# Sums of v over four blocks at a time, in a kernel that mixes a Fourier layer with sliding-window attention

## The chip, the cores and the metric

The kernel runs on one core of one Trainium2 chip. The metric is the device time of one execution in microseconds (us). Engines are named as the profile names them: PE is TensorE (PEld its weight loads), DVE VectorE, ACT ScalarE, POOL GpSimd, SP SyncE, whose queue issues most DMAs.

## The reference

The input x has 2048 rows of 512. Two mixers work on it, and a gate of each row blends them:

```python
g = sigmoid((x * gate_w).sum(-1))                     # one number for each row
a = x @ dft_hid_re.T ;  b = x @ dft_hid_im.T
y = dft_seq_re @ a - dft_seq_im @ b                   # Fourier mixer, 2048 x 2048 matrices
q, k, v = split(x @ wqkv)                             # 32 heads of 16
p = softmax(q @ k.T / 4, over the last 256 rows)      # causal sliding window
out = g * y + (1 - g) * ((p @ v) @ wo)
```

All of it is float32. The kernel splits each factor of a dense product into a rounded high part and a rest, and multiplies high by high, high by rest and rest by high (`TERMS`), so each dense product costs three matmuls.

## The kernel before

**Two streams on TensorE.** The order of TensorE's instructions is written by hand; that of the other engines and of the DMA queues is made by a scheduler, except where the code pins an instruction: `behind("sp")` issues what follows not before the last instruction that was marked on that queue, and `late(...)` the same for ScalarE and VectorE. The *dense stream* (`dense`, a generator) gives one 128 x 512 matmul at a time: projections of q, k and v for head group 0, of q and k for groups 1 to 3, the b projections (between groups 1 and 2) and the a projections of x (after group 3), then the products with the 2048 x 2048 matrices (`c_block`, "dc"), and near the end the output projection (`wo_block`). The *attention stream* is the loop over n at the end. It has 4 head groups x 32 blocks of 64 rows = 128 blocks. In step n, for four pairs p of a group's heads, it issues

- `s_pair(n, p)`: S, scores of queries against 320 keys. VectorE adds the mask and takes the row extreme (L329), ScalarE does the exponential and its sum (L332);
- `t_pair(k, p)` with k = n - LAG: T, the same scores transposed, with the row maxima as additional rows of the contraction. ScalarE takes the exponential into the tile `pt` (L393), GpSimd clears what lies outside the window (L398, L402);
- `pv`: the sums of v, products of `pt` with a padded v (`vpad`), four matmuls of 32 columns side by side for each block and bank (L419, "o"). I call a run of them a *visit*;
- between these, `fill(n)` lets matmuls of the dense stream in, 3.0 to 3.6 for each call pair.

S, T and the maxima's transposes share four PSUM banks (`ps_a`).

**Rings and pads.** q and k are stored to DRAM by the projections (`qk_scr`) and loaded 512 rows at a time into two ring tiles (`ring_load`, four DMAs). `ring_ahead` decides in which step: for group g and part ss the load waits for n - LAG >= 32 (g - 1) + 8 ss + 9, so that T no longer needs the rows that are overwritten. `make_pad` cuts a block out of a ring into a pad tile, one block ahead of its use; there are NPAD pads of each kind.

**Maxima and row sums.** After each eight blocks `m_rows` transposes their maxima on TensorE (L339), VectorE splits them, a DMA stores them (`m_scr`), and a second DMA, which waits for the first, loads them into four rows of the q ring for T. `l_rows` does the like for the row sums.

**v.** `v_load` loads v of four blocks into a raw tile, two steps later `v_spread` has GpSimd copy it into `vpad`, and three steps after that the first block of the four is summed.

**The gate.** `gate_load` loads 256 rows of x, `gate` multiplies them with gate_w and sums over the row on VectorE (L211).

Of the kernel before, what the change touches and what calls it, by code (L numbers as in the profile page):

```python
# [14 lines left out]
P = 128  # L15
# [9 lines left out]
SCALE = 0.25  # L25
LAG = 18
WARM = 6
BEHIND = 4
# [4 lines left out]
def fnet_window_mix(ctx: ExitStack, tc: tile.TileContext, xT, x, wqk, wv, wr, wi, cr, ci, wo, gw, out):  # L33
# [21 lines left out]
    def ld(dst, src):  # L55
        return nc.sync.dma_start(dst, src)

    def store(dst, src):
        mark("sp", ld(dst, src))

# [64 lines left out]
    def pt_raw():  # L125
        return at.tile([P, NP, WIN], F32, name="pt", bufs=3).rearrange("p a b -> p (a b)")[:, :1024]

    with tc.manual_schedule(engines={mybir.EngineType.Activation, mybir.EngineType.DVE, mybir.EngineType.SP}):
        wraw, *xraw = [pt_raw() for _ in range(3)]
        wq0 = [st.tile([P, 1024], F32R, name=h) for h in ("hi", "lo")]  # L130
        zero = at.tile([P, 512], F32R, name="rl", bufs=1)
        nc.vector.memset(f(zero[:]), 0.0)
        for dk in (0, 2, 1, 3):
            XRAW[dk, 0] = xraw[dk // 2][:, HALVES[dk % 2]]
            if dk % 2 == 0:
                nc.scalar.dma_start(XRAW[dk, 0], xT[0, dk])
        for dk in range(DK):
            store(wraw[:, dk * 256:dk * 256 + 256], wqk[0][:, dk * 256:dk * 256 + 256])
            if dk % 2 == 0:
                ld(XRAW[dk + 1, 0], xT[0, dk + 1])  # L140
        for dk in range(DK):
            c = slice(dk * 256, dk * 256 + 256)
            mark("act", nc.scalar.copy(wq0[0][:, c], wraw[:, c]))
            split_x(0, (dk,), dk > 0)
            mark("dve", nc.vector.tensor_sub(wq0[1][:, c], wraw[:, c], f(wq0[0][:, c])))


    NPAD = 3
    pads = [[const.tile([P, NP, P], F32R, name=f"pad{i}_{b}") for b in range(NPAD)] for i in range(2)]
# [14 lines left out]

    half = const.tile([P, 2], F32, name="half")
    mrow = const.tile([P, 2], F32, name="mrow")
    for t, edges in ((half, ((0, 16, 32, 48, 64, 80), (16, 32, 48, 64, 80, 96))), (mrow, ((96, 98), (98, 100)))):
# [13 lines left out]
    clear_rows(0, 0)  # L181
    vpad = [const.tile([P, 4, NP, 32], F32, name=f"vpad{b}") for b in range(2)]

# [12 lines left out]
    g0 = const.tile([P, 16], F32, name="g0")  # L196
    gwb = const.tile([P, D], F32, name="gwb")

    GX = {}

    def gate_load(j):
        if j == 0:
            with behind("sp"):
                ld(gwb, bass.AP(tensor=gw.tensor, offset=gw.offset, ap=[[0, P], [1, D]]))
        GX[j] = st.tile([P, 1024], F32, name="raw", bufs=2)
        for c in range(2):
            ld(GX[j][:, HALVES[c]], x[2 * j + c])

    def gate(tb):
        t = GX[tb // 2][:, HALVES[tb % 2]]  # L210
        nc.vector.scalar_tensor_tensor(t, t, 1.0, gwb, op0=OP.mult, op1=OP.mult,  # L211
                                       accum_out=gl[:, tb:tb + 1])
        if tb == 15:
            e = const.tile([P, 16], F32, name="ge")
            nc.scalar.activation(e, gl, AF.Exp, scale=-1.0)
            nc.vector.tensor_scalar_add(e, e, 1.0)
            nc.vector.reciprocal(g1, e)
            nc.vector.tensor_scalar(g0, g1, -1.0, 1.0, op0=OP.mult, op1=OP.add)
# [4 lines left out]
    def qk_evict(g, ss, i, ps):  # L223
        hl = ev.tile([P, 2, 512], F32R, name="hl", bufs=2)
        split_psum(hl[:, 0], hl[:, 1], ps, -SCALE if i == 0 else 1.0)
        store(qk_scr[i][g][ss].rearrange("h x s -> x h s"), f(hl[:]))

# [46 lines left out]
    def v_proj(sb, w):  # L274
        ps = ps_d.tile([P, 512], F32, name="dv", tag="d")
        yield from row_proj(sb, w, ps)
        t = ev.tile([P, 512], F32, name="ev")
        mark("act", nc.scalar.copy(t, ps))
        store(v_scr[sb // 2][sb % 2].rearrange("r a g x -> r (a g x)"), t)
        yield  # L280
# [6 lines left out]
    def ab_proj(i, sb, w, dst=None):  # L287
        ps = ps_d.tile([P, 512], F32, name="dab", tag="d")
        yield from row_proj(sb, w, ps)
        if dst is None:  # L290
            hl = ev.tile([P, 2, 512], F32R, name="hl", bufs=2)
            split_psum(hl[:, 0], hl[:, 1], ps, 1.0 if i == 0 else -1.0)
            store(ab_scr[i][sb], f(hl[:]))
        else:
            split_psum(dst[:, 0], dst[:, 1], ps)
        yield
# [38 lines left out]
    def m_rows(u):  # L335
        U = u % 4
        nm = ML[u][0]
        pt = ps_a.tile([P, 512], F32, name="s", tag="st")
        nc.tensor.matmul(pt[:32, :P], nm, ident, start=True, stop=True)  # L339
        hl = at.tile([32, 2, 2, 64], F32R, name="mhl", bufs=1)  # L340
        m = pt[:32, :P].rearrange("c (a r) -> c a r", a=2)
        nc.vector.tensor_scalar(hl[:, :, 0], m, -1.0, None, op0=OP.mult)
        nc.vector.scalar_tensor_tensor(hl[:, :, 1], m, -1.0, f(hl[:, :, 0]), op0=OP.mult, op1=OP.subtract)
        ld(m_scr[u].rearrange("x p (j r) -> (p j) x r", r=64), f(hl[:]).rearrange("c a h r -> c (a h) r"))
        ld(f(ring[0][96:100, :, U * 512:(U + 1) * 512]), m_scr[u])

    def l_rows(u):
        l = ML.pop(u)[1]
        nc.vector.reciprocal(l, l)
        pt = ps_a.tile([P, 512], F32, name="s", tag="st")  # L350
        nc.tensor.matmul(pt[:32, :P], l, ident, start=True, stop=True)  # L351
        lt = at.tile([32, P], F32, name="lt", bufs=1)
        nc.vector.tensor_copy(lt, pt[:32, :P])
        for a in range(2):
            ls = l_scr[u]
            ld(bass.AP(tensor=ls.tensor, offset=ls.offset + a * 512, ap=[[1024, NP], [64, 8], [1, 64]]),
               lt[:, 64 * a:64 * a + 64])
# [7 lines left out]
    def v_load(n):  # L365
        if n >= NG * NB:
            return
        g, kb = divmod(n, NB)
        raw = at.tile([P, 4, 64], F32, name="vr")
        for h in range(2):  # L370
            ld(raw[64 * h:64 * h + 64].rearrange("r (c j) x -> r c j x", j=2),
               v_scr[kb // 4][:, :, h, g, :].rearrange("c (j r) x -> r c j x", r=64))
        VR[n] = raw

    def v_spread(n):
        if n >= NG * NB:
            return
        raw = VR.pop(n)
        v2 = vpad[n // 4 % 2]
        for h in range(2):  # L380
# [4 lines left out]
    def t_pair(n, p):  # L385
        q0 = n % NB * BQ
        w = min(WIN, S - q0)
        if p == 0:
            PT[n] = at.tile([P, NP, WIN], F32, name="pt", bufs=3)
        pt = PT[n]  # L390
# [101 lines left out]
    def dense():  # L492
        warm()
        with behind("sp"):
            wraw = [load_raw(wv[i]) for i in range(2)]
        qk_first(wq0)
        wvs = [late(split_raw, r, True) for r in wraw]
        load_x(1, 0)
# [20 lines left out]
        for g in range(1, NG):  # L519
            for ss in range(4):  # L520
                yield from qk_proj(g, ss, w)
                have.add(("qk", g, ss))
                if g == 1:
                    if ss == 0:
                        wraw.append(load_raw(wi[1]))
                    elif ss < 3:
# [3 lines left out]
                        if ss == 1:  # L530
                            raw = load_raw(wqk[2])
                        else:
                            gate_load(0)
                elif g == 2:
# [10 lines left out]
            if g == 1:  # L545
                for sb in range(16):
                    yield from ab_proj(1, sb, ws)
                    if sb == 1:
                        nextw = late(split_raw, raw)
                    if sb % 2 == 0 and sb < 14:  # L550
                        gate_load(sb // 2 + 1)
                    if sb % 2:
                        late(gate, sb - 1)
                        late(gate, sb)
            if g < 3:
                w = nextw
        ab = {}
        for sb in range(16):
            if sb >= 4:
                ab[sb] = big.tile([P, 2, 512], F32R, name="big")  # L560
            yield from ab_proj(0, sb, ws, ab.get(sb))
        for sc in range(4):
            ab[sc] = load_ab(0, sc)
# [109 lines left out]
    ctx.enter_context(tc.manual_schedule(engines={mybir.EngineType.PE}))  # L673
    N = NG * NB
    need(("qk", 0, 0))
    ring_ahead(0)
    need(("v", 5))

    for n in range(N + LAG + 2):
# [6 lines left out]
        ring_ahead(n + 1)  # L686
        if -4 <= k < N - 4 and k % 4 == 0:
            for c in range(2):
                need(("v", (k + 4) % NB // 2 + c))
            with behind(*(("sp",) if k < 4 else ())):  # L690
                v_load(k + 4)
        if -4 <= k and k % 4 == 2:
            v_spread(k + 2)
        if n == 0:
            make_pad(0, 0)
        for p in range(NP):
# [9 lines left out]
            fill(n)  # L706
            if p == 2 and n % 2:
                for j in (k - 2, k - 1):
                    if 0 <= j < N:
                        pv(j)  # L710
                if n % 8 == 1 and 1 < n <= N + 1:
                    m_rows(n // 8 - 1)
                    l_rows(n // 8 - 1)
    attention_done()
# [46 lines left out]
```

## Time and profile before

| | us |
|---|---|
| median of three runs | 878.73 (878.17 to 880.12) |
| the profiled execution | 880.74 |
| its span, first to last instruction | 878.9 |
| PE busy | 868.7 (99%) |
| DVE busy | 601.4 (68%) |
| ACT busy | 583.6 (66%) |
| POOL busy | 386.6 (44%) |

The profile is of one execution. A row of a group or of the timeline names the line, the engine, the operation and the tiles (out<-in). In the timeline the first column is the start and the second the length; matmuls are pipelined and their lengths modelled, so it is the distance from start to start that tells TensorE's pace. A stretch's row (`A:B`) gives its length, the busy time of PE, PEld, DVE, ACT and POOL, the granted clock of TensorE, the DMA engines' busy share and GB/s.

### The profile page before, as it was taken

What the parts mean: (1) busy time and instruction counts of PE and PEld (TensorE: products, weight loads), DVE (VectorE), ACT (ScalarE), POOL (GpSimd) and SP (SyncE); (2) the same over time, 40 slices, a digit from 0 to 9 for tenths busy, and PEclk for the clock granted to TensorE, in tenths of its full rate; (3) what the DMA queues carried; (4) which work ended last, traced back from release to release, by engine and by line L of the source; (5) the groups of instructions that cost most, each with busy time, mean ns of one, the idle gap of its engine ahead of it and who ended that gap; (6) DMA issues with size and microseconds to landing.
All of it is one profiled execution on the core that took longest, in us unless ns stands there. A gap on an engine that the chain in (4) does not pass through costs nothing.

```text
span 878.9 us, 17233 instructions
## 1 busy us (share of the span) xinstructions
PE 868.7 (99%) x5190; PEld 694.0 (79%) x5190; DVE 601.4 (68%) x1968; ACT 583.6 (66%) x1793; POOL 386.6 (44%) x1069
## 2 busy tenths in 40 slices
PE   8999989999999999999999999999999999999998
PEld 6888867777878778787878787878787777788886
DVE  3588969777888678777877677878686434644341
ACT  3478978879898887888887878888786444110000
POOL 9100246454544447665456565645656665100000
PEclk9999999999999999999999999999999999999999
DMA  6877678675676126635445454469842425565531
GB/s 227 264 216 200 203 230 264 233 256 194 185 241 215 44 71 210 166 111 146 140 137 134 138 152 134 129 193 332 267 155 94 139 85 171 174 201 173 181 120 48
DMA packets 90541, 153.17 MB, mean 174 GB/s; under 512 B 26832, under 2 KB 35792, under 8 KB 90448
## 3 DMA queue, kind: packets, MB, share of 16 engines
q1 hardware_dynamic: 90016, 151.42, 55.1%
q8 instruction: 41, 0.67, 0.3%
q10 hardware_dynamic: 432, 0.66, 0.2%
q14 instruction: 52, 0.43, 0.2%
HBM read 104.33 MB, written 47.71 MB: 173 GB/s over the span
## 4 chain that ended last, share of the span: by engine, by line
PE 97%; DMA 1%; DVE 0%; issue 0%; ACT 0%; DVEq 0%; ACTq 0%
PE dc L450 41%; PE dab L268 10%; PE s L327 9%; PE dqk L246 9%; PE o L419 8%; PE t L392 8%; PE dv L268 5%; PE t L638 5%; DMA qk_scr<-hl 1%; PE s L234 1%; PE s L351 0%; DMA pt<-xT 0%; PE s L339 0%; ACT pt L393 0%; DVE lo L84 0%
## 5 line engine op out<-in xcount | busy, mean ns | idle before, releaser
L450 PE MATMUL dc<-big,hi 128*128 128x512 f32 x1024 | 354.8, 395 | 0.0
L398 POOL TENSOR_SCALAR_AFFINE_SELECT pt<-pt 64x128 f32<-64x128 f32 x512 | 194.3, 379 | 291.1 <-ACT pt L393 275.2
L332 ACT ACTIVATE sm<-sm,nm 128x320 f32<-128x320 f32 (+4 forms) x512 | 276.8, 542 | 56.8 <-DVE nm L329 54.1
L329 DVE CUSTOM_DVE_ANT_0 sm<-s,mask 128x320 f32<-128x320 f32 (+4 forms) x512 | 232.3, 462 | 114.9 <-PE s L327 88.5
L393 ACT ACTIVATE pt<-t 128x320 f32<-128x320 f32 (+4 forms) x512 | 207.9, 412 | 76.0 <-PE t L392 73.9
L450 PEld LDWEIGHTS dc<-big,hi 128*128 128x128 f32 x1024 | 186.9, 188 | 27.8 <-issue 1.5
L450 PE MATMUL dc<-big,lo 128*128 128x512 f32 x512 | 202.6, 396 | 0.0
L402 POOL TENSOR_SCALAR_AFFINE_SELECT pt<-pt 64x128 f32<-64x128 f32 x448 | 161.1, 360 | 0.0
L327 PE MATMUL s<-ring,pad 128*128 128x320 f32 (+4 forms) x512 | 160.4, 313 | 0.0
L392 PE MATMUL t<-ring,pad 128*128 128x320 f32 (+4 forms) x512 | 154.5, 302 | 2.9 <-ACT pt L393 2.9
L312 DVE TENSOR_SCALAR pad<-ring,half 96x256 fp32r<-96x256 f32 x384 | 121.8, 359 | 19.6 <-PE t L392 19.2
L327 PEld LDWEIGHTS s<-ring,pad 128*128 128x128 f32 x512 | 96.2, 188 | 38.7 <-issue 8.8
L392 PEld LDWEIGHTS t<-ring,pad 128*128 128x128 f32 x512 | 96.2, 188 | 20.4 <-ACT pt L393 4.0
L450 PEld LDWEIGHTS dc<-big,lo 128*128 128x128 f32 x512 | 96.2, 188 | 16.4 <-issue 1.6
L84 DVE TENSOR_TENSOR lo<-raw,hi 128x512 fp32r<-128x512 f32 x146 | 99.6, 713 | 0.0
L332 ACT ACTIVATION_READ_ACCUMULATOR sm<-sm,nm 128x1 f32 x512 | 98.2, 192 | 0.0
L268 PE MATMUL dab<-hi,big 128*128 128x512 f32 x256 | 92.1, 400 | 0.0
L83 DVE CAST hi<-raw 128x512 fp32r<-128x512 f32 x142 | 56.5, 438 | 43.4 <-PE dc L450 42.6
L246 PE MATMUL dqk<-big,hi 128*128 128x512 f32 x240 | 85.9, 393 | 0.0
L419 PE MATMUL o<-pt,vpad 128*32 128x320 f32 (+4 forms) x1408 | 78.5, 353 | 0.0
L81 ACT CAST os<-ev 128x512 fp32r<-128x512 f32 x16 | 9.8, 621 | 84.9 <-DMA ev<-o_scr 80.7
L419 PEld LDWEIGHTS o<-pt,vpad 128*32 128x32 f32 x1408 | 35.9, 109 | 37.2 <-issue 20.1
(83 smaller groups left out, 827.8 us busy)
## 6 DMA issues: line engine op xcount, KB each, us to landing
qk_scr<-hl SPq DMA_DIRECT2D x32, 512.0 KB
ring<-qk_scr SPq DMA_DIRECT2D x32, 512.0 KB
raw<-cr SPq DMA_DIRECT2D x32, 512.0 KB
raw<-ci SPq DMA_DIRECT2D x32, 512.0 KB
ab_scr<-hl SPq DMA_DIRECT2D x20, 512.0 KB
big<-ab_scr SPq DMA_DIRECT2D x20, 512.0 KB
ring<-qk_scr SPq DMA_DIRECT2D x32, 256.0 KB
r_scr<-ev SPq DMA_DIRECT2D x27, 256.0 KB
```

The costliest lines, as they stand in the source:

```text
L246: nc.tensor.matmul(ps, w[a][:, c:c + 128], XT[dk, ss][:, b], start=n == 0, stop=n == 11)
L268: nc.tensor.matmul(ps, XT[dk, ss][:, a, c * 128:(c + 1) * 128], wh[b], start=n == 0, stop=n == 11)
L312: nc.vector.tensor_scalar(dst, src, half[:96, h:h + 1], None, op0=OP.mult)
L327: nc.tensor.matmul(ps[:, :w], PAD[0, n][:, p], ring[1][:, p, k0:k0 + w], start=True, stop=True)
L329: mark("dve", nc.vector.tensor_tensor_reduce(out=sm[:, :w], in0=ps[:, :w], in1=mask[:, WIN - w:], scale=1.0, scalar=3e38, op0=OP.add, op1= ...
L332: mark("act", nc.scalar.activation(sm[:, :w], sm[:, :w], AF.Exp, bias=nm[:, c], scale=-1.0, accum_out=l[:, c]))
L392: nc.tensor.matmul(ps[:, :w], PAD[1, n][:, p], ring[0][:, p, q0:q0 + w], start=True, stop=True)
L393: nc.scalar.activation(pt[:, p, :w], ps[:, :w], AF.Exp, scale=-1.0)
L398: nc.gpsimd.affine_select(a, a, pattern=[[0, 2], [1, 64]], compare_op=OP.is_ge, fill=0.0, base=0, channel_multiplier=-1)
L402: nc.gpsimd.affine_select(a, a, pattern=[[0, 2], [-1, 64]], compare_op=OP.is_gt, fill=0.0, base=0, channel_multiplier=1)
L419: nc.tensor.matmul(OT[g, sb][32 * p:32 * p + 32, q - sb * 512:e - sb * 512], v2[:, p], pt[:, p, q - q0:e - q0], start=first, stop=kb == 8 ...
L450: nc.tensor.matmul(ps, w[a][:, s8 * 128:(s8 + 1) * 128], ab[SC[i]][:, b], start=i == 0 and a + b == 0, stop=i == 15 and a == 1)
```

## The change

- **Visits.** The sums of v are made at p = 2 of each step with k a multiple of 4, four blocks at a time, where before they were made at odd n, two blocks at a time. `pt` has five buffers instead of three.
- **LAG** is 21 instead of 18: T runs 21 blocks behind S.
- **Room** for it: NPAD 2 instead of 3, one `vpad` instead of two, one raw v tile instead of two; the small tile of the row sums and the gate's weights come out of the pool `ev`; `half` and `mrow` share a tile; the DMA scratch is 512 bytes instead of 1024.
- **v loads** for blocks k to k + 3 are issued in step n = k + LAG (before: those for k + 4 to k + 7), all pinned behind SP's last DMA. Every load is now marked on SP's queue, not only the stores.
- **Maxima.** The load of the maxima into the ring is issued from ScalarE's queue, one step after the visit in which they were transposed, pinned behind ScalarE's last marked instruction.
- **Gate.** Its loads and products move from the b projections, two products at each second of 16 row blocks, to the a projections, two products at each of the row blocks 2 to 9.
- **Start.** WARM is 8 instead of 6, and the v weights' splits stand ahead of the first q and k projection's evictions (ScalarE's order is now: four casts of the v weights, then the two evictions).

```diff
-LAG = 18
-WARM = 6
+LAG = 21
+WARM = 8
...
     def ld(dst, src):
-        return nc.sync.dma_start(dst, src)
-
-    def store(dst, src):
-        mark("sp", ld(dst, src))
+        mark("sp", nc.sync.dma_start(dst, src))
...
-    NPAD = 3
+    NPAD = 2
...
-    vpad = [const.tile([P, 4, NP, 32], F32, name=f"vpad{b}") for b in range(2)]
+    vpad = [const.tile([P, 4, NP, 32], F32, name="vpad")]
...
         if j == 0:
+            gwb.append(ev.tile([P, D], F32, name="ev"))
             with behind("sp"):
-                ld(gwb, bass.AP(tensor=gw.tensor, offset=gw.offset, ap=[[0, P], [1, D]]))
+                ld(gwb[0], bass.AP(tensor=gw.tensor, offset=gw.offset, ap=[[0, P], [1, D]]))
...
-        ld(f(ring[0][96:100, :, U * 512:(U + 1) * 512]), m_scr[u])
+
+    def m_ring(u):
+        U = u % 4
+        with behind("act"):
+            nc.scalar.dma_start(f(ring[0][96:100, :, U * 512:(U + 1) * 512]), m_scr[u])
...
-        lt = at.tile([32, P], F32, name="lt", bufs=1)
+        lt = ev.tile([P, 512], F32, name="ev")[:32, :P]
...
-        raw = at.tile([P, 4, 64], F32, name="vr")
+        raw = at.tile([P, 4, 64], F32, name="vr", bufs=1)
...
-        v2 = vpad[n // 4 % 2]
+        v2 = vpad[0]
...
-            PT[n] = at.tile([P, NP, WIN], F32, name="pt", bufs=3)
+            PT[n] = at.tile([P, NP, WIN], F32, name="pt", bufs=5)
...
+        wvs = [late(split_raw, r, True) for r in wraw]
         qk_first(wq0)
-        wvs = [late(split_raw, r, True) for r in wraw]
...
-                    if sb % 2 == 0 and sb < 14:
-                        gate_load(sb // 2 + 1)
-                    if sb % 2:
-                        late(gate, sb - 1)
-                        late(gate, sb)
...
             yield from ab_proj(0, sb, ws, ab.get(sb))
+            if sb < 10:
+                if sb < 8:
+                    gate_load(sb)
+                if sb > 1:
+                    late(gate, 2 * sb - 4)
+                    late(gate, 2 * sb - 3)
...
-        if -4 <= k < N - 4 and k % 4 == 0:
+        if 0 <= k < N and k % 4 == 0:
             for c in range(2):
-                need(("v", (k + 4) % NB // 2 + c))
-            with behind(*(("sp",) if k < 4 else ())):
-                v_load(k + 4)
-        if -4 <= k and k % 4 == 2:
-            v_spread(k + 2)
+                need(("v", k % NB // 2 + c))
+            with behind("sp"):
+                v_load(k)
+        if 0 <= k and k % 4 == 2:
+            v_spread(k - 2)
...
-            if p == 2 and n % 2:
-                for j in (k - 2, k - 1):
+            if p == 2 and sent < maxima:
+                m_ring(sent)
+                sent += 1
+            if p == 2 and k % 4 == 0:
+                for j in range(k - 4, k):
                     if 0 <= j < N:
                         pv(j)
-                if n % 8 == 1 and 1 < n <= N + 1:
-                    m_rows(n // 8 - 1)
-                    l_rows(n // 8 - 1)
+                if maxima < 16 and n > 8 * maxima + 8:
+                    m_rows(maxima)
+                    l_rows(maxima)
+                    maxima += 1
```

More of the change, by code (lines that the diff above doesn't have):

```diff
@@ L125, in pt_raw @@
     def pt_raw():
-        return at.tile([P, NP, WIN], F32, name="pt", bufs=3).rearrange("p a b -> p (a b)")[:, :1024]
+        return at.tile([P, NP, WIN], F32, name="pt", bufs=5).rearrange("p a b -> p (a b)")[:, :1024]
     with tc.manual_schedule(engines={mybir.EngineType.Activation, mybir.EngineType.DVE, mybir.EngineType.SP}):
@@ L137, in fnet_window_mix @@
         for dk in range(DK):
-            store(wraw[:, dk * 256:dk * 256 + 256], wqk[0][:, dk * 256:dk * 256 + 256])
+            ld(wraw[:, dk * 256:dk * 256 + 256], wqk[0][:, dk * 256:dk * 256 + 256])
             if dk % 2 == 0:
@@ L163, in fnet_window_mix @@
                             base=0, channel_multiplier=-1)
-    half = const.tile([P, 2], F32, name="half")
-    mrow = const.tile([P, 2], F32, name="mrow")
+    cols01 = const.tile([P, 4], F32, name="cols01")
+    half, mrow = cols01[:, 0:2], cols01[:, 2:4]
     for t, edges in ((half, ((0, 16, 32, 48, 64, 80), (16, 32, 48, 64, 80, 96))), (mrow, ((96, 98), (98, 100)))):
@@ L196, in fnet_window_mix @@
     g0 = const.tile([P, 16], F32, name="g0")
-    gwb = const.tile([P, D], F32, name="gwb")
+    gwb = []
     GX = {}
@@ L210, in gate @@
         t = GX[tb // 2][:, HALVES[tb % 2]]
-        nc.vector.scalar_tensor_tensor(t, t, 1.0, gwb, op0=OP.mult, op1=OP.mult,
+        nc.vector.scalar_tensor_tensor(t, t, 1.0, gwb[0], op0=OP.mult, op1=OP.mult,
                                        accum_out=gl[:, tb:tb + 1])
@@ L225, in qk_evict @@
         split_psum(hl[:, 0], hl[:, 1], ps, -SCALE if i == 0 else 1.0)
-        store(qk_scr[i][g][ss].rearrange("h x s -> x h s"), f(hl[:]))
+        ld(qk_scr[i][g][ss].rearrange("h x s -> x h s"), f(hl[:]))
     def qk_first(w):
@@ L278, in v_proj @@
         mark("act", nc.scalar.copy(t, ps))
-        store(v_scr[sb // 2][sb % 2].rearrange("r a g x -> r (a g x)"), t)
+        ld(v_scr[sb // 2][sb % 2].rearrange("r a g x -> r (a g x)"), t)
         yield
@@ L292, in ab_proj @@
             split_psum(hl[:, 0], hl[:, 1], ps, 1.0 if i == 0 else -1.0)
-            store(ab_scr[i][sb], f(hl[:]))
+            ld(ab_scr[i][sb], f(hl[:]))
         else:
@@ L531, in dense @@
                             raw = load_raw(wqk[2])
-                        else:
-                            gate_load(0)
                 elif g == 2:
@@ L674, in fnet_window_mix @@
     N = NG * NB
+    maxima = sent = 0
     need(("qk", 0, 0))
@@ L752 @@
     arrays = {k: np.ascontiguousarray(v) for k, v in arrays.items()}
-    nc = bacc.Bacc("TRN2", target_bir_lowering=False, num_devices=1, dynamic_dma_scratch_size=1024)
+    nc = bacc.Bacc("TRN2", target_bir_lowering=False, num_devices=1, dynamic_dma_scratch_size=512)
     args = [nc.dram_tensor(k, v.shape, mybir.dt.from_np(v.dtype), kind="ExternalInput").ap()
```

## The prediction

> **What bounds the kernel now.** I read the page first (busy shares, the chain of waits that ended last), then the timeline of TensorE around one visit to the sums of v, then the stretches in which TensorE is not at its pace.
>
> ```profile
> span 878.9 us, 17233 instructions
> PE 868.7 (99%) x5190; PEld 694.0 (79%) x5190; DVE 601.4 (68%) x1968; ACT 583.6 (66%) x1793; POOL 386.6 (44%) x1069
> PE 97%; DMA 1%; DVE 0%; issue 0%; ACT 0%; DVEq 0%; ACTq 0%
> ```
>
> TensorE is busy for 99% of the span and carries 97% of the chain: the time is the length of TensorE's instruction stream, and every microsecond must come out of that stream or be added to it. No matmul of the work is removed. What can change is the spacing between matmuls, so I look for places where one start lies further from the next than its columns need.
>
> ```profile
> 106.94 0.39 PE L246 MATMUL dqk<-big,hi 128*128 128x512 f32 x1
> 107.26 0.75 PE L419 MATMUL o<-pt,vpad 128*32 128x320 f32 x8
> 107.93 0.41 PE L327 MATMUL s<-ring,pad 128*128 128x320 f32 x1
> 108.19 0.40 PE L246 MATMUL dqk<-big,hi 128*128 128x512 f32 x1
> ...
> 162.53 0.39 PE L268 MATMUL dab<-hi,big 128*128 128x512 f32 x1
> 162.84 1.28 PE L419 MATMUL o<-pt,vpad 128*32 128x320 f32 x16
> 164.06 0.41 PE L327 MATMUL s<-ring,pad 128*128 128x320 f32 x1
> 164.31 0.39 PE L268 MATMUL dab<-hi,big 128*128 128x512 f32 x1
> ```
>
> The first column is the start, the second the modelled length; starts tell the pace. `o` is the sum of v (L419): four 32-column matmuls run side by side, so x8 is two groups and x16 four groups of 320 columns. Two groups occupy 107.26 to 107.93 = 0.67 us, four 162.84 to 164.06 = 1.22 us, so a group costs 0.275 us and each visit 0.12 us beside its groups. Before it, the last 512-wide matmul holds TensorE 0.31 to 0.32 us; behind it, the next 320-wide S matmul holds it 0.25 to 0.26 us. The normal paces follow from:
>
> ```profile
> 308.82 0.39 PE L268 MATMUL dab<-hi,big 128*128 128x512 f32 x1
> 309.05 0.31 PE L327 MATMUL s<-ring,pad 128*128 128x320 f32 x1
> 309.20 0.39 PE L268 MATMUL dab<-hi,big 128*128 128x512 f32 x1
> ```
>
> That is 0.23 us for 512 columns and 0.15 us for 320. So a visit costs 0.09 us on entry, 0.12 us inside and 0.11 us behind it: 0.32 us, whatever it sums (0.30 us by the second visit).
>
> **The visits (the main term).** Before, odd blocks n = 19 to 147 make 65 visits. After, k = 4, 8, ... 128 make 32, with the same 1408 `o` matmuls. 33 x 0.32 = 10.6 us off TensorE's stream, none of it hidden behind anything. Bounds: 9.9 us (0.30 each) and 11.2 us (0.34, the same 0.02 us the other way).
>
> **The start.** The v weights' splits now stand ahead of the evictions of the first q and k on ScalarE and VectorE.
>
> ```profile
> 12.12 1.28 ACT L87 ACTIVATE hl<-s 128x512 fp32r<-128x512 f32 x2 [3.50 <-PE s L234]
> 13.30 2.17 ACT L81 CAST hi<-raw 128x512 fp32r<-128x512 f32 x4
> ...
> 12.38 0.39 PE L234 MATMUL s<-big,lo 128*128 128x512 f32 x1
> 13.96 0.49 PE L268 MATMUL dv<-hi,big 128*128 128x512 f32 x1 [1.19 <-ACT hi L81]
> 14.78 0.50 PE L268 MATMUL dv<-lo,big 128*128 128x512 f32 x1 [0.32 <-DVE lo L84]
> ...
> 19.46 0.63 PE L268 MATMUL dv<-hi,big 128*128 128x512 f32 x2
> ...
> 12.00:15.80 3.80, 2.28 (x9) 1.35 (x8) 3.05 (x5) 3.26 (x6) 3.67 (x4) 1.00 0.38 141
> 15.80:19.20 3.40, 3.40 (x10) 2.60 (x9) 0.73 (x2) 0.24 (x1) 3.30 (x4) 0.51 0.98 300
> ```
>
> ScalarE sits idle for 3.50 us until the q and k are there and only then casts; TensorE waits for that cast. From 12.38 to 19.46 there are 15 starts in 7.08 us; at 0.23 us they need 3.45 us: 3.6 us are lost. Of these 13.96 - 12.38 - 0.23 = 1.35 and 14.78 - 13.96 - 0.23 = 0.59 us are the wait; the rest, 1.7 us, is a granted clock of 0.51 between 15.8 and 19.2, right behind a stretch in which TensorE was busy for 2.28 of 3.80 us. With the wait gone I expect the clock to stay up. I take 3.3 us of the 3.6, leaving 0.3 us for VectorE's own split, which is next in line. The bound from below is 1.9 us, if the clock falls all the same. The Trainium skill (TensorE: Matmul & The Clock Gate, Part 1) says that the clock is halved after a whole idle window of about 3.4 us. By that rule a stretch that was 60% busy should not have done it, and the drop would stay: an estimate of 1.9 us for the start. The trace shows the drop after only two short gaps, so I follow the row. Two more warm-up matmuls I count at nothing: TensorE spends that time waiting for VectorE's first split of x anyway; without this cover they cost 2 x 0.23 / 0.51 = 0.9 us.
>
> **The first T blocks.**
>
> ```profile
> 115.20 0.39 PE L246 MATMUL dqk<-big,lo 128*128 128x512 f32 x1
> 117.93 0.41 PE L392 MATMUL t<-ring,pad 128*128 128x320 f32 x1 [2.35 <-ACT pt L393]
> ...
> 105.00:115.00 10.00, 10.00 (x55) 7.67 (x54) 8.94 (x32) 7.90 (x25) 5.42 (x12) 1.00 1.04 262
> 115.00:121.00 6.00, 3.65 (x11) 2.39 (x10) 2.63 (x8) 4.04 (x13) 3.34 (x12) 0.78 1.07 348
> ```
>
> Here TensorE stalls 2.5 us and then runs at a clock of 0.78 on average (about 1.1 us more): 3.6 us. The DMA share in these stretches (second to last figure) is 1.04 and 1.07, so the DMA engines are full: stores, ring loads, the first v loads and the first gate loads meet. The change takes the gate loads out and starts T three blocks later. But the ring load for S block 24, tied to LAG, is now issued three blocks ahead instead of six, into the same crowd. I take half, 1.8 us saved; ends 3.6 us saved and 3 us lost.
>
> **Maxima through ScalarE's queue.** The load of the maxima waits for their store, and what waits on ScalarE's queue holds all exponentials behind it, then T and the sums.
>
> ```profile
> 307.20 0.38 PE L339 MATMUL s<-ident,nm 128*32 128x128 f32 x2
> 308.93 0.38 SPq L56 DMA_DIRECT2D m_scr<-mhl  x1
> 310.73 0.62 SPq L56 DMA_DIRECT2D ring<-m_scr  x1
> ...
> 600.02 0.38 SPq L56 DMA_DIRECT2D m_scr<-mhl  x1
> 607.45 0.66 SPq L56 DMA_DIRECT2D ring<-m_scr  x1
> ```
>
> The store is issued 1.7 us after the maxima's transpose and the load could be issued 3.5 us after it. The new place is one block later, 5 us, plus ScalarE's lag behind TensorE, so mostly nothing is left to wait for. The worst row (607.45, 7.4 us behind its store) would hold ScalarE some 4 us, once. Sixteen issues of about 0.62 us also take 10 us of ScalarE, in its slack. I add 0.8 us, between 0 and 6. The Trainium skill (DMA: Bandwidth & Descriptors, Issuing engines are not separate DMA queues) says a second issuing engine saves only issue time, since all transfers share 16 DMA engines. It would make this move worth nothing; I count no gain either.
>
> **The gates.** They move from the b projections, two for each pair of blocks of rows, to the a projections, two for each single one.
>
> ```profile
> L211 DVE SCALAR_TENSOR_TENSOR raw<-raw,gwb 128x512 f32<-128x512 f32 x16 | 10.7, 707 | 0.0
> L211 DVE DVE_READ_ACCUMULATOR raw<-raw,gwb 128x1 f32 x16 | 1.3, 80 | 0.0
> 260.00:330.00 70.00, 70.00 (x456) 55.94 (x455) 51.07 (x182) 61.44 (x196) 32.09 (x106) 1.00 0.39 118
> ```
>
> Sixteen cost 12.0 us of VectorE. The a projections are this stretch, 16 steps in 70 us; eight steps take the gates, 35 us, where VectorE already has 0.73 x 35 = 25.5 us. The sum is 37.5 of 35 us: VectorE is 2.5 us short there, less what it now idles during visits. I add 1 us (0 to 3). No price is recovered in the b projections, where VectorE hid the gates.
>
> **The visits' own cover.** A visit needs the last masked exponentials of the block before.
>
> ```profile
> 304.68 0.30 POOL L402 TENSOR_SCALAR_AFFINE_SELECT pt<-pt 64x128 f32<-64x128 f32 x1
> 306.09 1.29 PE L419 MATMUL o<-pt,vpad 128*32 128x192 f32 x32
> ```
>
> They are ready 1.1 us ahead here. ScalarE is busy 61.44 of 70 us, and it catches up while TensorE sums. With visits twice as far apart it builds its backlog over four blocks: 0.88 x 5.15 (the time of a block, below) = 4.53 us of work for a block that TensorE, without its visit, passes in (10.30 - 1.22 - 0.20) / 2 = 4.44 us, so 0.4 us behind in four blocks, 1.0 us with the maxima's issue. That nearly eats the cover in the projections; I add 1.5 us over all visits (0 to 8). A single v pad and one raw buffer cost nothing: they are filled two blocks behind the visit that frees them and two ahead of the next.
>
> **The ring loads.** Their distance to use shrinks from six blocks to three.
>
> ```profile
> 25.59 0.56 SPq L56 DMA_DIRECT2D ring<-qk_scr  x1
> 34.76 0.61 DVE L312 TENSOR_SCALAR pad<-ring,half 96x256 fp32r<-96x256 f32 x2
> ...
> 311.40 0.59 SPq L56 DMA_DIRECT2D ring<-qk_scr  x1
> ...
> 339.97 0.19 PE L327 MATMUL s<-ring,pad 128*128 128x64 f32 x1
> ```
>
> S block 58 starts at 309.05 (above) and the q parts are issued by 312.0, 2.9 us into it; block 64, which uses them, starts at 339.97: 30.9 us for six blocks, 5.15 us each. After the change they would be issued 2.9 us into block 61 and needed when the pad of block 64 is made, at the start of block 63, 10.3 us in. That leaves 7.4 us for the loads to land. The very first ring load, issued at 25.59 among others, was used at 34.76, so it took at most 9.2 us: late by at most 1.8 us, twelve times, and VectorE being late is felt by TensorE only two pairs on (the banks between them), some 2 us. I add 0.5 us, between 0 and 14.
>
> **Sum.** -10.6 - 3.3 - 1.8 + 0.8 + 1.0 + 1.5 + 0.5 = -11.9 us. The profiled execution took 880.7 us (span 878.9, 1.8 us around it), 2.0 us above the median of 878.73. 880.7 - 11.9 = 868.8, on the median's scale 866.8: **867 us**. The end of the kernel, sixteen blocks of the output projection spread over the last four steps instead of the last five, has the same matmuls and the same last store, behind the same c block: nothing; if the preparation of the first four were late, 1 to 3 us.
>
> **Rivals.** *All of the lost time comes back and nothing new waits*: -10.6 - 3.6 - 3.6 gives 863 and 861 us on the median's scale. For it: TensorE waits nearly nowhere else. Chance 0.12. *ScalarE's backlog takes the place of the visits' cost*: at 0.25 us late in each of 32 visits, 8 us come back, 873 to 875 us. For it: the cover of 1.1 us; against: in the second half ScalarE is less busy. Chance 0.14. *The cost belongs to pairs of blocks, not visits* (the drain is paid at each change of accumulation bank): then only start and first T blocks gain, -5.1 + 2.3 = -2.8 us, 876 us; against it stand the rows of two and four groups above. Chance 0.04. *Slower*: the ring loads land late. Place: the pad of blocks 32, 40, ... 120, twelve times. If the queue of SP is held for half the 7.4 us of the row at 607.45 and a load takes 9.2 us, it lands 2.9 + 3.7 + 9.2 = 15.8 us into block 61, 3 us beyond the 10.3 us and the 2.5 us that two pairs give; twelve of these are 36 us, and the time is about 903 us. It turns the sign from 12 / 12 = 1.0 us each. Against: loads of k are issued much earlier, and only two of four parts are tight. Chance 0.07.
>
> **Numbers.** The forecast 867 us has 0.63, its own range 863 to 872. The range 860 to 877 leaves out the ring rival, the tail of the backlog rival and part of the fourth, under 0.2. A measurement of this kernel can tell about 0.2%, 1.8 us. Faster: 0.63 + 0.12 + 0.13 = 0.88; same 0.04; slower 0.08.
>
> **What would show it.** Right: `o` rows of x32 at least, TensorE's pitch around them unchanged at 0.09 and 0.11 us; no gap between the first q, k and the v projection and a clock of 1.00 from 12 to 20 us; waits of TensorE under 5 us in total. Wrong: waits of S or T on the pads or on ring loads, `o` on the masked exponentials, or idle ScalarE ahead of its own load of the maxima.

## The result, and the profile after

| | median | runs |
|---|---|---|
| before | 879.67 us | 22 (878.17 to 880.98) |
| after | 878.35 us | 22 (875.27 to 880.55) |
| ratio | 0.9985 | 95% interval 0.9978 to 0.9991 |

The change gains 1.3 us, a ninth of the 12 us that were forecast; 878.35 us lies above the range (860 to 877). The profiled execution after took 879.21 us, with a span of 877.5 us.

The page of the kernel after, from its parts 1 and 4:

```profile
span 877.5 us, 17233 instructions
PE 860.5 (98%) x5192; PEld 694.9 (79%) x5192; DVE 602.1 (69%) x1966; ACT 581.4 (66%) x1793; POOL 393.9 (45%) x1066
PE 91%; DVE 3%; DMA 3%; ACT 1%; issue 1%; SPq 0%; ACTq 0%; DVEq 0%
```

TensorE's share of the chain fell from 97% to 91%, and DMA and VectorE took its place: TensorE has less to do (860.5 us against 868.7) and now waits. What it waits for, in the waits of TensorE after (us in total, times, longest):

```profile
PE t L394 <- DVE nm L327: 2.5, 1, 2.5
PE s L325 <- DVE pad L310: 2.2, 1, 2.2
PE s L325 <- DVE nm L327: 2.0, 1, 2.0
```

Single waits of 2 us or more are what one looks for here. VectorE's waits name what stands behind them: the first line is the kernel before, the second the kernel after.

```profile
DVE pad L312 <- DMA ring<-qk_scr: 0.2, 1, 0.2
DVE pad L310 <- DMA ring<-qk_scr: 6.0, 3, 3.2
```

The pads of S wait for ring loads. The first place, in the timeline after around S block 24, with the stretch behind it:

```profile
110.17 3.22 SPq L56 DMA_DIRECT2D ring<-qk_scr  x4
120.02 0.88 DVE L310 TENSOR_SCALAR pad<-ring,cols 96x256 fp32r<-96x256 f32 x3 [3.21 <-DMA ring<-qk_scr]
121.36 0.46 PE L394 MATMUL t<-ring,pad 128*128 128x320 f32 x1 [2.54 <-DVE nm L327]
...
121.00:125.00 4.00, 3.64 (x11) 3.09 (x12) 2.80 (x10) 2.85 (x9) 3.18 (x10) 0.57 0.56 223
```

The ring loads, issued from 110.17 on, hold VectorE until 120.02. The maxima of S, queued behind the pad on VectorE, then hold T for 2.54 us, and TensorE runs at a clock of 0.57 for 4 us. The second place, around block 120; the row with 11.13 is the chain's own piece:

```profile
595.43 1.28 SPq L56 DMA_DIRECT2D ring<-qk_scr  x2
...
610.09 1.19 SPq L56 DMA_DIRECT2D ring<-qk_scr  x2
610.68 11.13 DMA ring<-qk_scr
621.90 0.63 DVE L310 TENSOR_SCALAR pad<-ring,cols 96x256 fp32r<-96x256 f32 x2 [2.57 <-DMA ring<-qk_scr]
...
614.00:627.00 13.00, 8.82 (x34) 6.58 (x33) 8.23 (x28) 6.75 (x21) 5.06 (x17) 0.87 0.66 162
```

The k parts go out at 595.43, the q parts only 14.7 us later, and the last lands 11.13 us after its issue. S block 117 starts at 602.83, so the q parts go out 7.3 us into it; the q parts of blocks 32 to 112 go out within 0.5 us of the start of the block that releases them. By the semaphore updates in the trace, the issue at 610.09 had waited for the reload (`big<-ab_scr`) issued at 598.76, whose last part landed at 610.03: the landing of an earlier transfer held SP's queue. Of 13 us TensorE works 8.82, at a clock of 0.87. In the kernel before, the same 13 us read:

```profile
614.00:627.00 13.00, 13.00 (x75) 10.32 (x75) 8.61 (x33) 11.04 (x37) 7.40 (x22) 1.00 1.04 369
```

What was promised did come. A visit after, and the start:

```profile
154.71 0.40 PE L266 MATMUL dab<-hi,big 128*128 128x512 f32 x1
155.04 2.38 PE L421 MATMUL o<-pt,vpad 128*32 128x256 f32 x64
157.35 0.41 PE L325 MATMUL s<-ring,pad 128*128 128x320 f32 x1
157.60 0.40 PE L266 MATMUL dab<-hi,big 128*128 128x512 f32 x1
...
11.70 0.39 PE L232 MATMUL s<-big,lo 128*128 128x512 f32 x1
11.93 0.39 PE L266 MATMUL dv<-hi,big 128*128 128x512 f32 x1
...
12.00:15.80 3.80, 3.80 (x19) 3.14 (x18) 1.66 (x3) 1.32 (x3) 3.54 (x5) 1.00 0.90 245
15.80:19.20 3.40, 3.40 (x17) 2.81 (x16) 0.49 (x1) 1.63 (x3) 3.40 (x3) 1.00 1.03 399
```

Visits hold x64 (four blocks) with 0.33 us on entry and 0.25 us behind, as before. The v projection follows q and k without a gap, and the clock stays at 1.00.

All starts of TensorE, each set against the pace of its columns, give the whole account of the two spans (us):

| | before | after |
|---|---|---|
| lost in the first 20 us | 7.9 | 3.0 |
| visits: entry, sums, behind | 84.4 | 72.7 |
| stalls (over 0.06 us each, lost clock included) | 11.5 | 25.9 |
| all else | 775.1 | 775.8 |
| span | 878.9 | 877.5 |

So 16.6 us were gained and 14.4 us came back as stalls.

### The profile page after: what moved, and what is told of

Same layout as the page of the kernel before. It is cut to its first block, busy times and chain, and to the rows that moved or that the text cites. A ratio compares the mean times of both kernels' runs of the same rounds, so it can differ in the third digit from the quotient of the medians.

```text
span 877.5 us, 17233 instructions
## 1 busy us (share of the span) xinstructions
PE 860.5 (98%) x5192; PEld 694.9 (79%) x5192; DVE 602.1 (69%) x1966; ACT 581.4 (66%) x1793; POOL 393.9 (45%) x1066
## 4 chain that ended last, share of the span: by engine, by line
PE 91%; DVE 3%; DMA 3%; ACT 1%; issue 1%; SPq 0%; ACTq 0%; DVEq 0%
PE dc L452 40%; PE dab L266 9%; PE s L325 8%; PE o L421 8%; PE dqk L244 8%; PE t L394 7%; PE dv L266 5%; PE t L639 5%; DMA ring<-qk_scr 2%; DVE sm L327 1%; ACT sm L330 1%; DVE pad L310 1%; DMA pt<-wqk 0%; PE s L232 0%; DVE lo L81 0%
## 5 line engine op out<-in xcount | busy, mean ns | idle before, releaser
L400 POOL TENSOR_SCALAR_AFFINE_SELECT pt<-pt 64x128 f32<-64x128 f32 x512 | 189.3, 370 | 305.0 <-ACT pt L395 285.9
L404 POOL TENSOR_SCALAR_AFFINE_SELECT pt<-pt 64x128 f32<-64x128 f32 x448 | 174.6, 390 | 0.0
L325 PE MATMUL s<-ring,pad 128*128 128x320 f32 (+4 forms) x512 | 157.4, 307 | 5.1 <-DVE pad L310 2.2
L310 DVE TENSOR_SCALAR pad<-ring,cols 96x256 fp32r<-96x256 f32 x384 | 121.7, 356 | 27.1 <-PE t L394 18.5
L80 DVE CAST hi<-raw 128x512 fp32r<-128x512 f32 x142 | 59.5, 459 | 46.1 <-PE dc L452 40.0
L421 PE MATMUL o<-pt,vpad 128*32 128x320 f32 (+4 forms) x1408 | 71.5, 350 | 0.0
L308 ACT ACTIVATE pad<-ring,cols 96x256 fp32r<-96x256 f32 x128 | 64.1, 501 | 0.0
L421 PEld LDWEIGHTS o<-pt,vpad 128*32 128x32 f32 x1408 | 37.7, 110 | 29.2 <-issue 9.3
```

Of the source, the lines that this page charges most:

```text
L310: nc.vector.tensor_scalar(dst, src, half[:96, h:h + 1], None, op0=OP.mult)
L325: nc.tensor.matmul(ps[:, :w], PAD[0, n][:, p], ring[1][:, p, k0:k0 + w], start=True, stop=True)
L400: nc.gpsimd.affine_select(a, a, pattern=[[0, 2], [1, 64]], compare_op=OP.is_ge, fill=0.0, base=0, channel_multiplier=-1)
L404: nc.gpsimd.affine_select(a, a, pattern=[[0, 2], [-1, 64]], compare_op=OP.is_gt, fill=0.0, base=0, channel_multiplier=1)
L421: nc.tensor.matmul(OT[g, sb][32 * p:32 * p + 32, q - sb * 512:e - sb * 512], v2[:, p], pt[:, p, q - q0:e - q0], start=first, stop=kb == 8 ...
```

## The experiments

**Theory:** the ring loads, whose lead over their use fell from 6 blocks to 3 with the lag of 21, land late at two crowded places, and this took most of the gain. **Rivals:** ScalarE's queue with the maxima; the gates; the long visits themselves; or a short lead that does harm everywhere. Where two kernels ran in different sets, they are compared by their ratios to the kernel before (1% is 8.8 us).

**Half loads of the ring.**

```
-        while loaded < 16:
-            g, ss = divmod(loaded, 4)
+        while loaded < 28:
...
-            if ("qk", g, ss) not in have or n - LAG < 32 * (g - 1) + 8 * ss + 9:
+            if ("qk", g, ss) not in have or g and n - LAG < 32 * (g - 1) + 8 * ss + hi // 64 + 1:
```

Here `lo` and `hi` are 0 and 512 in group 0, and then 0 and 256, 256 and 512 in turn; `ring_load` loads the columns from `lo` to `hi`.

> The changed kernel with only the ring loads' release changed: for groups 1 to 3 each load is cut into two of 256 columns, and a half is released as soon as the T blocks that read those 256 columns are issued; the loads of group 0, which nothing has read before, go as soon as q and k are there. The lead of a load over the S block that needs it goes from 3 blocks to 7, at 21 blocks of lag, with 24 more DMA issues in each queue direction. Theory (the short lead took the gain): the stalls of TensorE at 118 to 127 us and at 610 to 627 us go, VectorE's waits for ring<-qk_scr ahead of the pads go with them, and the time falls by 8 to 10 us against the changed kernel, to about 869. Rival (ScalarE's backlog or the visits themselves): those two places stay, no more than 2 us are gained. Rival (SP's queue is what delays the loads, not the release): the loads of the third group still land late at 615 us, the gain is 3 us (the place at 118 alone).

Measured: 868.14 us, ratio 0.9869 (0.9856 to 0.9883): 10.2 us less than the kernel after. VectorE no longer waits for a ring load anywhere, and the two places read, in the stretches of this kernel (block 117 starts at 596.58 here, so the second place is in the last two):

```profile
121.00:125.00 4.00, 3.24 (x16) 2.54 (x16) 4.00 (x12) 4.00 (x15) 2.50 (x8) 1.00 0.86 289
608.00:614.00 6.00, 4.75 (x21) 3.50 (x22) 5.59 (x21) 4.61 (x16) 2.28 (x8) 1.00 0.64 185
614.00:627.00 13.00, 13.00 (x89) 9.96 (x88) 9.14 (x34) 9.58 (x32) 6.90 (x19) 1.00 0.23 78
```

A short wait is left at each place, 0.76 us at 123.52 and 1.31 us at 609.12, neither for a ring load. With the visits, the lag and the maxima's queue untouched, the ring loads alone give the time back. This run changes both their release and, in groups 1 to 3, their size; the next one changes the release alone.

**Group 0 alone.** Only the `g and` of the diff above, with whole loads.

> The changed kernel with one condition dropped: the ring loads of group 0, which no T block has read before them, no longer wait for T and go as soon as q and k are projected (in the changed kernel the fourth of them waits until block 21, 3 blocks ahead of its use). Groups 1 to 3 as changed. Theory (two places of short lead, about 4 us at 118 to 127 us and about 6 us at 610 to 627 us): the first place goes, the second stays, 4 us less than the changed kernel, about 874.4. Rival (one place only matters, and what half loads gained was at 610 us): within 1 us of 878.4. Rival (the whole gain of the half loads was here): about 868.

Measured: 873.56 us, ratio 0.9926 (0.9913 to 0.9939): 5.2 us less than after, by the release alone; the 5.0 us between this kernel and half loads are left for groups 1 to 3, so the two places are worth about 5 us each. The second stays, in this kernel's timeline:

```profile
617.00 0.61 DVE L310 TENSOR_SCALAR pad<-ring,cols 96x256 fp32r<-96x256 f32 x2 [3.98 <-DMA ring<-qk_scr]
617.66 0.41 PE L325 MATMUL s<-ring,pad 128*128 128x320 f32 x1 [3.53 <-DVE pad L310]
```

**The same without the reloads.** Is it the lead, or the crowd?

```
-                        nxt[SC[k]] = load_ab(1, SC[k])
+                        nxt[SC[k]] = ab[SC[k]]
```

> The changed kernel with group 0's ring loads free of T, and without the 16 reloads of the second projection's tiles (big<-ab_scr from 573 to 604 us): the second pass computes with the tiles of the first, so its values are others, with the same matmuls. The lead of the last ring load stays at 3 blocks. Theory (3 blocks are too few only where the reloads crowd the DMA engines and SP's queue): the stalls at 608 to 621 us go without any change of the lead, 5 us less than with the reloads (873.6), about 868.5, and the last ring load lands within 7 us. Rival (the lead alone does it): within 1 us of 873.6.

This kernel leaves out the 16 reloads, so its output is another; the matmuls are the same. Measured: 867.36 us, ratio 0.9856 (0.9837 to 0.9876), 6.2 us less than with the reloads. VectorE's whole wait for ring loads:

```profile
DVE pad L310 <- DMA ring<-qk_scr: 0.3, 1, 0.3
```

The q parts now go out 0.3 us ahead of block 117 and land in 7.3 and 7.6 us; with the reloads they went out 7.1 us into it and took 10.9 and 11.8 us. So three blocks are enough without the reloads, and at this place short lead and crowd are both needed: the larger part of the delay is the late issue, the smaller the slower landing. At the first place only the lead was tried.

**The lag alone, on the kernel before** (`LAG = 21`, nothing else).

> The kernel before with one number changed: T 21 blocks behind S in place of 18, so that ring loads are released 3 blocks ahead of their use in place of 6; visits, start, maxima, v loads and gate as before. Theory (the short lead costs about 10 us at two places; the first T blocks, 3.8 us of stalls between 110 and 120 us in the kernel before, may change by 2 or 3 either way): 7 to 12 us more than before, 887 to 892, with VectorE waiting for ring<-qk_scr ahead of pads near 120 and 615 us. Rival (the lead costs only together with visits of four blocks or single v buffers): within 2 us of the kernel before.

Measured: 890.89 us, ratio 1.0123 (1.0106 to 1.0141): 10.8 us more. VectorE's wait, and three of the places, in the waits and the timeline of this kernel:

```profile
DVE pad L312 <- DMA ring<-qk_scr: 17.5, 15, 2.9
...
63.72 0.61 DVE L312 TENSOR_SCALAR pad<-ring,half 96x256 fp32r<-96x256 f32 x2 [2.63 <-DMA ring<-qk_scr]
...
126.54 1.40 DVE L312 TENSOR_SCALAR pad<-ring,half 96x256 fp32r<-96x256 f32 x5 [2.85 <-DMA ring<-qk_scr]
...
633.18 1.21 DVE L312 TENSOR_SCALAR pad<-ring,half 96x256 fp32r<-96x256 f32 x4 [2.82 <-DMA ring<-qk_scr]
```

The size was as expected, the places only in part: 15 waits, at the pads of blocks 8 and 16 as well, not two. This kernel has three pads of each kind, and VectorE comes to a pad a block earlier (read from the two traces, not tried alone). It waits for the pad of block 40 in block 38, until 207.97; the changed kernel, with two pads, makes that pad at 203.23, at the start of block 39 and 5.0 us after the load has landed. The sum of stalls rose by 10.1 us (11.5 to 21.6). Late ring loads are the mechanism of the rival *Slower*, and here the kernel is slower; but they are late at other places than in the changed kernel, so that the size comes near the 10.2 us of half loads is in part chance.

**A lag of 17.**

> The changed kernel with T 17 blocks behind S in place of 21, everything else kept; the visits stay on the same blocks of S (n mod 4 = 1). Ring loads are released 7 blocks ahead of their use in place of 3, with unchanged issues. Theory (the short lead took the gain): the same 8 to 10 us as with half loads, to about 869; the maxima now have 3 blocks (some 17 us) from their load to the first T that reads them, which is enough. Rival (maxima by ScalarE's queue land too late): T waits at blocks 8u - 4, 15 times, for the load of the maxima, and the time is above 878. Rival (the lag is not the cause): within 2 us of the changed kernel's 878.4.

Measured: 881.93 us, ratio 1.0028 (1.0018 to 1.0037): 3.8 us more than after, against the theory. VectorE's waits for ring loads are gone here too. In their place ScalarE waits, once:

```profile
ACT sm L330 <- DMA big<-ab_scr: 7.1, 1, 7.1
```

The transfer named is a reload. In the timeline of this kernel:

```profile
601.67 0.32 SPq L56 DMA_DIRECT2D m_scr<-mhl  x1
605.87 0.52 SPq L56 DMA_DIRECT2D big<-ab_scr  x1
610.90 0.64 ACTq L347 DMA_DIRECT2D ring<-m_scr  x1
611.59 0.56 ACT L330 ACTIVATE sm<-sm,nm 128x320 f32<-128x320 f32 x1 [7.05 <-DMA big<-ab_scr]
```

The exponential stands behind ScalarE's own load of the maxima, issued at 610.90. What that load reads, stored at 601.67, had landed by 607.35, going by the semaphore updates in the trace. The load was still held by the semaphore of the reload issued at 605.87, whose last update comes at 610.83. So for the second half of its 7.1 us ScalarE stood idle for a transfer that its load does not read.

**A lag of 17, maxima by SP's queue.**

> T 17 blocks behind S and the maxima's loads back on SP's queue; everything else as changed. With 17 blocks and ScalarE's queue the time was 881.9: there ScalarE stood idle for 7.1 us ahead of its load of the maxima at 610.9 us, whose source was stored at 601.7 us into the crowd of reloads. Theory (ScalarE's queue was blocked by that wait, 4.3 us of TensorE and the clock after it): about 6 to 8 us less than 881.9, 874 to 876. Rival (the stall at 608 us is the crowd itself, whoever issues the load): within 2 us of 881.9.

Measured: 885.56 us, ratio 1.0066 (1.0051 to 1.0081): slower still, against both. In the waits of TensorE:

```profile
PE t L393 <- DMA ring<-m_scr: 8.2, 1, 8.2
PE t L393 <- DVE nm L327: 5.0, 1, 5.0
```

On SP's queue that wait of ScalarE is gone, but the load of the maxima, issued at 612.56, lands 10.5 us later, and T waits for it itself. A smaller lag gives the ring loads lead and takes it from the maxima (7 blocks to 3), and here the crowd finds them. ScalarE's queue is not what makes a lag of 17 slow: without it the time is longer.

**Maxima by SP's queue, at 21; then with half loads.**

```
-        with behind("act"):
-            nc.scalar.dma_start(f(ring[0][96:100, :, U * 512:(U + 1) * 512]), m_scr[u])
+        ld(f(ring[0][96:100, :, U * 512:(U + 1) * 512]), m_scr[u])
```

> The changed kernel with the 16 loads of the maxima into the ring back on SP's queue (still one step after they are stored); everything else as changed. Theory (ScalarE's queue costs nothing, since ScalarE is not idle ahead of them): within 1 us of 878.4. Rival (16 x 0.64 us of ScalarE are on the path): up to 6 us less, about 872 to 876.

> Half loads of the ring and the maxima's loads back on SP's queue, everything else as changed. Theory (the two gains add: 10.2 and 1.6 us against the changed kernel): 1.6 us less than half loads alone, about 866.5, ahead of both kernels. Rival (the 1.6 us of SP's queue came from where the short ring loads landed, and go with them): within 0.5 us of 868.1.

Measured: 876.74 us, ratio 0.9972 (0.9961 to 0.9982), 1.1 us less than after, with overlapping intervals; with half loads 868.30 us, ratio 0.9867 (0.9853 to 0.9880), against 0.9869 without. The queue is worth nothing that these runs can tell.

**Gates back in the b projections; then with half loads.** The three places of the gate's code as in the kernel before.

> The changed kernel with the gate's loads and its 16 multiply-and-sums back in the b projections, as they stood before the change; everything else as changed. Theory (the gates on VectorE in the a projections cost about 4 us, from the stalls between 250 and 310 us): 4 us less than the changed kernel, about 874.4, and the stalls at 274 to 278 us gone. Rival (they only changed which engine is named late): within 1 us of 878.4. Rival (they cost as much in the b projections, where the T blocks run as well): same or slower than 878.4.

> Half loads of the ring, and the gate's loads and sums back in the b projections as before; everything else as changed. Theory (with the ring loads out of the way the gate costs about 2 us more in the a projections than in the b projections): 2 us less than half loads alone (868.1), about 866. Rival (it costs the same in both): within 0.7 us of 868.1.

Measured: 878.49 us, ratio 0.9996 (0.9984 to 1.0008), and 867.63 us, ratio 0.9859 (0.9842 to 0.9875). The first profile (883.24 us, the longest of its runs) shows fewer stalls from 250 to 310 us (2.4 us in place of 4.4), as expected, and 3.5 us more from 110 to 180 us, where the gates now stand and the ring load of block 24 is late. With the ring loads out of the way, the difference to half loads alone lies within both intervals. My 4 us for the gates, read off the stalls of one stretch, were wrong.

**The start alone, on the kernel before** (`WARM = 8`, the splits of the v weights ahead of `qk_first`).

> The kernel before with one part of the change: the v weights' splits ahead of the evictions of the first q and k, and 8 warm-up matmuls in place of 6. Theory (the start gains by itself what the two traces' first 20 us differ by, 7.87 - 3.00 = 4.9 us): 4.9 us less than before, about 874.8, and the clock stays up between 15 and 20 us. Rival (the forecast's 3.3 us): about 876.4. Rival (the clock falls all the same): 1.9 us less or no gain.

Measured: 875.46 us, ratio 0.9948 (0.9935 to 0.9960): 4.6 us less than before. The clock between 15.8 and 19.2 us:

```profile
15.80:19.20 3.40, 3.40 (x17) 2.82 (x16) 0.51 (x1) 1.62 (x3) 3.34 (x2) 1.00 0.96 369
```

**Two blocks a visit, with half loads.**

```
-            if p == 2 and k % 4 == 0:
-                for j in range(k - 4, k):
+            if p == 2 and k % 2 == 0:
+                for j in range(k - 2, k):
```

> The changed kernel with half loads of the ring and, as in the kernel before, visits to the sums of v after every two blocks in place of four (65 in place of 32; v spread one block earlier). Theory (each visit costs 0.32 to 0.36 us, whatever it sums): 33 visits more cost 10.6 to 11.7 us over the kernel with half loads alone (868.1), about 879. Rival (the cost belongs to pairs of blocks): no more than 4 us over, about 872.

Measured: 877.05 us, ratio 0.9967 (0.9956 to 0.9977): 8.6 us more than half loads alone. There are 64 visits (k = 2, 4, ... 128), one fewer than expected. By the starts of TensorE, 32 visits more cost 11.3 us (entry 3.1 to 6.2, sums 67.7 to 72.5, behind 2.0 to 5.3): 0.35 us each. The stalls fell by 2.2 us (15.4 to 13.2), which is what the longer visits cost.

## Why the prediction was wrong

- **Ring loads: the step that failed.** The term was 0.5 us, with 14 as its end, for the pads of blocks 32 to 120; the ring load of block 24 was weighed with the first T blocks. Half loads measured the two together at 10.2 us, and group 0 alone parts them: 5.2 us for group 0, where the wait is at block 24, and 5.0 us for the rest. In that rest VectorE waits at one of the twelve pads, that of block 120. The rival *Slower* held the mechanism with a chance of 0.07, but at all twelve. The step took one landing time, 9.2 us, for all loads, added it to a regular issue 2.9 us into the block, and found each late by 1.8 us at most, which two pairs of cover would take. For most loads that was too dark: in the kernel after, the q parts of blocks 32 to 112 go out within 0.5 us of the start of the block, land in 4.7 to 7.4 us, and nothing waits. At block 120 it was far too bright: the issue came 7.3 us into block 117, behind the landing of a reload, and the landing took 11.13 us. Two rows pointed there: the load of the maxima issued at 607.45, 7.4 us behind its store, was read for the maxima, and a DMA share of 1.04 to 1.07 near 115 us for the first T blocks. To the loads of groups 1 to 3 the first was put only as a rival, for twelve equal loads rather than for the one that meets the reloads. The lost clock behind a stall was priced at the start and at the first T blocks, not here.
- **First T blocks: wrong sign.** Forecast 1.8 us saved, ends 3.6 saved and 3 lost. Stalls from 100 to 130 us went from 4.1 to 7.1 us: the lost end. It is the same fault (the ring load of block 24, issued from 3.5 us into block 21), which the text named and weighed at a half. With group 0 released early they are 3.1 us. The two terms together came out 9.3 us above the forecast (5.0 us lost for 0.5, and 3.0 us lost for 1.8 saved), of the 10.6 us between forecast and result. What the text gave as a sign of being wrong, waits of S on the pads, is among the waits of TensorE (2.2 us).
- **Visits: right, a little larger.** 0.32 us each was forecast (0.34 at most), 0.35 measured; 33 fewer are 11.7 us by starts. **Their cover**: 1.5 us forecast, 2.2 us measured in stalls; that ScalarE's backlog is what causes them was argued, not tested.
- **Start: right, larger.** 3.3 us forecast, 4.6 us by time and 4.9 us by starts. The wait and the clock drop went together. The Trainium skill (TensorE: Matmul & The Clock Gate, Part 1) asks for a whole idle window of about 3.4 us, by which only 1.9 us would have come; the trace does not agree, since the clock stayed at 1.00 once the gaps of 1.35 and 0.59 us were gone. Some 0.7 us more lies ahead of it: the last q and k matmul starts at 11.70, not 12.38. The warm-ups' share in that was not tried alone.
- **Maxima** (0.8 forecast) and **gates** (1.0): no cost that can be measured at a lag of 21. The sum would have said the same without them. The Trainium skill (DMA: Bandwidth & Descriptors, Issuing engines are not separate DMA queues) says that a second issuing engine saves only the time of issuing; both pairs of runs agree, with 876.74 against 878.35 us and 868.30 against 868.14 us.

The measured parts: -4.6 (start) - 8.6 (visits with their cover) + 10.2 (ring loads) = -3.0 us; the measurement is -1.3. The 1.7 us between are the distance from the start alone (0.9948) to half loads with two blocks a visit (0.9967): the price of the rest of the change, from the lag to the single buffers. The intervals of these two ratios overlap a little (0.9956 to 0.9960), and the rest was not taken apart. Half loads with the gates in the b projections, 867.63 us, are ahead of both kernels. That this comes near the forecast's 867 is in part chance: visits and start gained more than their terms, the first T blocks and the cover less.

## What to carry to other kernels

When a lag or a ring moves, list every transfer whose release hangs on it, and price each at its own place: issue as the queue of that moment lets it, landing as the DMA share of that moment lets it, and the slower clock behind a stall. A mean lead that suffices for fourteen loads says nothing of the two that meet a crowd. Release loads by what they overwrite (here 256 columns, and nothing at all for the first group) before giving up lead for something else, since a lag set smaller only hands the shortage to the next transfer.

## What was not expected of the hardware

The granted clock fell after short gaps: to 0.57 over 4 us behind a single stall of 2.54 us (121.36), and to a mean of 0.87 from 614 to 627 us. That is 1.7 us of lost clock at each place (0.43 x 4 and 0.13 x 13), of about 5 us. A ring load's landing went from 4.7 to 7.4 us to 11.13 us where the reloads and others held the DMA engines at a share of 1.04 (608 to 614 us).

A DMA issue waited for a transfer that has nothing to do with it. The q part of the ring load at 610.09 and, with a lag of 17, ScalarE's load of the maxima at 610.90 each went out 0.06 to 0.07 us after the last semaphore update of an earlier reload (610.03 and 610.83). In the traces each issue shares its semaphore with that reload and waits for it first. So a crowd delays the issue as well as the landing: here by 7.6 us, against some 4 us in the landing.
